# The first three loads of r change their issuing queue, from SyncE to ScalarE

## The chip, the cores and the metric

The kernel runs on one core of a Trainium2 chip. The metric is the device time of one execution in microseconds (us): the median over runs.

## The reference

Two layers follow each other. The first is a linear attention with a decaying state (4 batches, 8 heads, 768 steps, head size 48); the second is a two-layer MLP with a squared ReLU over the 3072 tokens, of width 384 and inner width 2048.

```
state = zeros(B, H, D, D)
for t in range(S):
    cur = einsum('bhd,bhe->bhde', u * k[:, :, t], v[:, :, t])
    y[:, :, t] = einsum('bhd,bhde->bhe', r[:, :, t], state + cur)
    state = w * state + einsum('bhd,bhe->bhde', k[:, :, t], v[:, :, t])
x = y as (B*S, H*D)
h = maximum(x @ moe_w_in, 0)
out = (h * h) @ moe_w_out
```

## The kernel before

The 768 steps are cut into 6 chunks of 128, and with 4 batches that makes 24 units, numbered i, unit i being chunk i // 4 of batch i % 4. For every unit three tiles of 128 steps x 8 heads x 48 values in float32 are loaded (`ld.r.i`, `ld.k.i`, `ld.v.i`, 192 KB each). A head's row of 48 values is contiguous in memory and nothing longer is, so each of these loads is 1024 pieces of 192 bytes.

Per unit the work is:

- `kh` and `rh` (L320, L323) scale k by `Wkhat` and r by `Wt` into a bf16 tile `rk`. Both factors are powers of the decay w. They are made once, at the start: the load `w` brings w's row (L256), `shw` spreads it over the partitions on VectorE (L265), and ScalarE forms `logw`, `Wkhat` and `Wt` (L271, L274, L277).
- `P0`, `P1`, `du`, `dv` (L326, L330, L333, L338) are the part with u.
- `T` transposes `rk` on TensorE (L347) and `Tc` copies the result to SBUF (L250). From unit 8 on a transposing DMA (`XB`, L353) does both.
- `A` is the 128x128 product of the two transposed tiles (L360), `Bm` masks it (L372), `Y` multiplies it and the state with v (L380, L382), and `U` makes the state's update (L391).
- `xs` adds Y and dv (L399), `X` transposes the sum (L417) and `xTc` copies it (L250); later units use a transposing DMA (`xX`, L424).
- `F1`, `re`, `sq`, `F2` are the MLP (L433, L441 and L443, L448 to L452, L460), for one unit or a pair of units at a time; `os` and `out` store the result.

The weights of the MLP come in eight pieces. Of `moe_w_in`, four pieces of 768 KB in rows of 2 KB are loaded in float32 (`lW.0.s`, L301) and cast to bf16 (`cW.0.s`: L250 on ScalarE, L252 on GpSimd). The four of `moe_w_out` are loaded by GpSimd's queue with a cast on the way (`W.1.s`, L317; 384 KB as written); a tiny copy, `gate` (L311), that reads a loaded v tile stands ahead of each and holds it back.

Nothing is scheduled by a program: the string `ORDER` lists all steps of all engines, and each engine carries out its own steps in the order in which they stand there. A step reads `name.numbers:engine/buffer`, with A for ScalarE, D for VectorE, G for GpSimd, P for TensorE and S for SyncE. SyncE (SP in the profile) only issues DMAs, and nearly all of them are its own: 24 loads each of r, k and v, the four `lW`, the stores and the transposing DMAs. ScalarE issues one DMA in the whole kernel, the row of w.

The r, k and v tiles have five buffers each; a load from the sixth unit on waits until its buffer's last readers are done. DMAs from SyncE and ScalarE draw their completion semaphores from eight that are reused in turn, so that the ninth such DMA also waits until the first one has landed, and so on.

Of the kernel before, what the change touches and what calls it, by code (L numbers as in the profile page):

```python
# [17 lines left out]
POOLS = dict(ldr=5, ldk=5, ldv=5, ws=4, rk=6, P0=4, dv=3, vb=8, rkT=6, bank=4, bankH=2, bankO=2, Bm=6, xs=3, xT1=2, xT2=2, xT4=1, hr=6, hq=28, os=3, ts=2)  # L18
GATES = [[('v', 1), ('v', 1), ('v', 1), ('v', 1)], [('v', 1), ('v', 1), ('v', 3), ('v', 3)]]
ORDER = """  # L20
tab:A ld.k.1:S/0 ld.r.0:S/0 ld.r.1:S/1 ld.k.0:S/1 w:A lW.0.2:S/0 u:S lW.0.0:S/1 lW.0.1:S/2 ld.v.1:S/0 shw:D ld.k.2:S/2
logw:A Wk:A ld.v.3:S/1 P0.1:D/0 Wt:A kh.1:G/0 ld.r.2:S/2 kh.0:D/1 rh.1:D rh.0:G ld.k.4:S/3 T.1:P/0 cW.0.2:A ld.v.4:S/2
P0.0:D/1 T.0:P/1 Tc.1:A/0 shu:D ld.r.3:S/3 P1.0:D Tc.0:A/1 P1.1:D A.1:P/2/3 du.0:D/0 cW.0.0:A A.0:P/0/1 du.1:D/1
ld.v.0:S/3 cW.0.1:G Bm.0.0:D/0 ld.k.3:S/4 Bm.0.1:D/1 vb.1:A/0 lW.0.3:S/3 Bm.1.1:D/2 kh.2:G/2 Bm.1.0:D/3 ld.v.2:S/4
gate.1.0:G vb.3:D/1 Y.1:P/0 wc:S U.1:P/1 gate.1.1:G dv.1:D ld.r.4:S/4 xs.1:D/0 P0.2:G/2 X.1:P/3 ld.k.5:S/0 vb.4:A/2
# [82 lines left out]
    ld=["{0}{1}"],  # L108
    lW=["ws{0}{1}"], kh=["rk{0}"], P0=["P{0}"], du=["dv{0}"], vb=["vb{0}"], T=["bT{0}"], Tc=["rkT{0}"], XB=["rkT{0}"],
# [413 lines left out]
```

## Time and profile before

| | |
|---|---|
| median of 13 runs | 183.52 us (181.42 to 185.4) |
| the profiled execution's own time | 184.97 us |
| its span in the profile | 183.3 us |
| TensorE matmul busy (PE) | 156.7 us, 86% |
| VectorE / ScalarE / GpSimd busy | 124.3 / 120.8 / 112.9 us |
| granted TensorE clock | full speed in all 40 slices |
| packets on the queue of SyncE (q1) | 103912, 27.81 MB |
| packets on the queue of ScalarE (q10) | 8, 0.01 MB |

The span is the time between the first and the last recorded instruction. The execution's own time has 1.67 us more around it. Rows of a timeline give the start and the duration in us, the engine and line, the tile written and the tile read, the number of instructions merged into the row, and in brackets the idle time before the row with what ended it. "SPq" and "ACTq" are DMA issues of SyncE and ScalarE: their duration is how long the issuing takes the queue's sequencer, not how long the data take. The DMA share is that of 16 DMA engines; it counts each packet with a duration of its own and so can come out above 100%.

### The profile page before, as it was taken

How to read it: one execution, taken by the hardware profiler on the slowest of the kernel's cores; microseconds unless marked ns; L12 is line 12 of the kernel's file. 1: busy time of each engine (PE TensorE's matmuls, PEld its weight loads, DVE VectorE, ACT ScalarE, POOL GpSimd, SP SyncE). 2: the span in 40 equal slices, each digit the busy share in tenths (PEclk: the TensorE clock that was granted, in tenths of full speed). 3: DMA queues.
4: the chain of work that ended last, by engine and by line, in shares of the span. 5: the costliest groups of instructions: out<-in, count | busy, mean ns of one | idle time of the engine just before them, and what ended most of it. 6: DMA issues, size and time to landing. Idle time of an engine off the chain costs nothing.

```text
span 183.3 us, 4254 instructions
## 1 busy us (share of the span) xinstructions
PE 156.7 (86%) x1640; PEld 118.5 (65%) x1640; DVE 124.3 (68%) x220; ACT 120.8 (66%) x209; POOL 112.9 (62%) x125
## 2 busy tenths in 40 slices
PE   0143677999799999878999998999999999999992
PEld 0032656768577777646777867668687787777761
DVE  3767289768868898876868587587984777723220
ACT  2374549678489857815759659749667776677852
POOL 3406687955596599882899996969989940000000
PEclk9999999999999999999999999999999999999999
DMA  5999999989799899989899899899755325220112
GB/s 111 267 337 183 190 250 200 209 151 200 155 212 231 200 179 223 146 195 199 189 179 209 181 191 192 168 214 150 165 117 123 60 66 122 68 64 0 50 40 86
DMA packets 106052, 29.66 MB, mean 162 GB/s; under 512 B 99368, under 2 KB 104496, under 8 KB 106032
## 3 DMA queue, kind: packets, MB, share of 16 engines
q1 hardware_dynamic: 103912, 27.81, 71.7%
q0 software_dynamic: 2112, 1.57, 5.8%
q8 instruction: 13, 0.21, 0.5%
q14 instruction: 7, 0.06, 0.1%
q10 hardware_dynamic: 8, 0.01, 0.0%
HBM read 20.46 MB, written 4.72 MB: 137 GB/s over the span
## 4 chain that ended last, share of the span: by engine, by line
PE 60%; DMA 19%; SPq 11%; ACT 3%; issue 2%; DVE 2%; POOL 1%; DVEq 0%; ACTq 0%
PE bank L460 27%; PE bank L433 26%; DMA ldv<-in_v_dram 13%; SPq L296 9%; DMA W<-in_moe_w_out_dram 5%; PE bank L382 2%; DMA xT<-xs 2%; PE bank L360 2%; ACT hr L441 2%; SPq L301 2%; PE bank L380 2%; PE bank L391 1%; DVE du L333 1%; ACT vb L250 1%; DVE rk L323 1%
## 5 line engine op out<-in xcount | busy, mean ns | idle before, releaser
L433 PE MATMUL bank<-xT,W 128*128 128x256 bf16 (+1 forms) x624 | 73.9, 268 | 4.1 <-ACT W L250 1.4
L460 PE MATMUL bank<-W,hq 128*128 128x384 bf16 x384 | 73.3, 326 | 1.4 <-DMA W<-in_moe_w_out_dram 0.9
L433 PEld LDWEIGHTS <-W 128*128 128x128 bf16 x624 | 57.0, 100 | 14.6 <-issue 2.4
L441 ACT ACTIVATE hr<-bank 128x512 bf16<-128x512 f32 x86 | 50.7, 595 | 23.3 <-PE bank L433 21.9
L460 PEld LDWEIGHTS <-hq 128*128 128x128 bf16 x384 | 36.1, 98 | 20.1 <-issue 1.3
L450 DVE TENSOR_TENSOR hq<-bank,hr 128x512 bf16<-128x512 f32 x37 | 25.4, 689 | 28.7 <-ACT hr L441 28.7
L448 ACT ACTIVATE hq<-hr 128x512 bf16<-128x512 bf16 x57 | 35.7, 629 | 1.9 <-DVE hr L443 0.4
L372 DVE TENSOR_TENSOR Bm<-bank,maskJT 128x512 bf16<-128x512 f32 x48 | 31.0, 681 | 3.3 <-PE bank L360 3.3
L326 POOL TENSOR_TENSOR P<-ldr,ldk 128x384 f32<-128x384 f32 x22 | 23.9, 1087 | 4.1 <-DMA ldr<-in_r_dram 4.1
L320 POOL TENSOR_TENSOR rk<-ldk,Wkhat 128x384 bf16<-128x384 f32 x21 | 21.3, 1015 | 4.4 <-ACT Wkhat L274 4.1
L323 POOL TENSOR_TENSOR rk<-ldr,Wt 128x384 bf16<-128x384 f32 x20 | 21.7, 1084 | 2.7 <-DMA ldr<-in_r_dram 2.7
L330 POOL TENSOR_TENSOR P<-P,ub 128x384 f32<-128x384 f32 x20 | 21.8, 1088 | 1.2
L250 ACT CAST vb<-ldv 128x384 bf16<-128x384 f32 x22 | 11.2, 509 | 17.1 <-DMA ldv<-in_v_dram 17.0
L412 POOL TENSOR_TENSOR S0W<-ts,WLm 128x384 bf16<-128x384 f32 x14 | 14.2, 1017 | 10.7 <-DVE ts L409 10.6
L399 DVE TENSOR_TENSOR xs<-bank,dv 128x384 bf16<-128x384 f32 x24 | 13.3, 552 | 7.2 <-PE bank L382 6.6
L250 ACT COPY os<-bank 128x384 f32<-128x384 f32 x22 | 10.4, 472 | 7.0 <-PE bank L460 6.7
L382 PE MATMUL bank<-vb,Bm 128*128 128x48 bf16 x192 | 11.4, 185 | 4.1 <-DVE Bm L372 2.6
L347 PE MATMUL bank<-identity,rk 128*128 128x128 bf16 x64 | 6.2, 254 | 9.0 <-POOL rk L320 7.6
L382 PEld LDWEIGHTS <-Bm 128*128 128x128 bf16 x192 | 9.8, 97 | 5.7 <-DVE Bm L372 2.9
L338 DVE TENSOR_TENSOR dv<-ldv,du 128x384 f32<-128x384 f32 x19 | 13.1, 692 | 0.3
L333 DVE TENSOR_REDUCE du<-P 128x8 f32<-128x384 f32 x24 | 12.9, 543 | 0.1
L360 PE MATMUL bank<-rkT 48*128 48x128 bf16 x192 | 8.6, 225 | 3.6 <-ACT rkT L250 2.4
(57 smaller groups left out, 111.9 us busy)
## 6 DMA issues: line engine op xcount, KB each, us to landing
ldk<-in_k_dram SPq DMA_DIRECT2D x24, 192.0 KB, 3.8
ldr<-in_r_dram SPq DMA_DIRECT2D x24, 192.0 KB, 3.7
ldv<-in_v_dram SPq DMA_DIRECT2D x24, 192.0 KB, 5.0
out_dram<-os SPq DMA_DIRECT2D x24, 192.0 KB, 2.9
ws<-in_moe_w_in_dram SPq DMA_DIRECT2D x4, 768.0 KB, 7.2
W<-in_moe_w_out_dram POOLq DMA_DIRECT2D x4, 384.0 KB, 7.9
rkT<-rk SPq DMA_TRANSPOSE x16, 3.5
xT<-xs SPq DMA_TRANSPOSE x16, 3.1
```

Of the source, the lines that this page charges most:

```text
L250: e.copy(o, a)
L320: e.tensor_mul(rk[slot[f"rk{i}"]][:, 1, :, 0:D], loaded("k", i), Wkhat)
L323: e.tensor_mul(rk[slot[f"rk{i}"]][:, 0, :, 0:D], loaded("r", i), Wt2)
L326: e.tensor_mul(P0b[slot[f"P{i}"]], loaded("r", i), loaded("k", i))
L330: e.tensor_mul(t, t, ub)
L372: e.tensor_mul(Bmb[slot[f"Bm{i}{h}"]], heads(bank(f"bA{i}{h}"), 128), mask_b)
L382: e.matmul(y[:, hc, D * h : D * (h + 1)], m[h][:, hc, :], vb[:, 2 * hc + h, :], start=(c == 0), stop=True, skip_group_check=True,)
L433: e.matmul(hp[:, fi, :], W1[f // 4][:, c, 128 * (f % 4) : 128 * (f % 4 + 1)], xt[:, c, :], start=(c == 0), stop=(c == CCH - 1), skip_group ...
L441: e.activation(hr, hp, AF.Relu)
L448: e.activation(hq, hr, AF.Square)
L450: e.tensor_mul(hq, bank(f"bH{g},{s}", "bH"), hr)
L460: e.matmul(bank(f"bO{i}", "bO")[:, 0:d_model], hqb[slot[f"hq{g},{f // m}"]][:, at : at + L], W2[q][:, f % 4, :], start=(f == 0), stop=(f = ...
```

## The change

`ld.r.0`, `ld.r.1` and `ld.r.2` are given to engine A. Buffers and places in `ORDER` stay as they are. No other line of the kernel changes.

```diff
 ORDER = """
-tab:A ld.k.1:S/0 ld.r.0:S/0 ld.r.1:S/1 ld.k.0:S/1 w:A lW.0.2:S/0 u:S lW.0.0:S/1 lW.0.1:S/2 ld.v.1:S/0 shw:D ld.k.2:S/2
-logw:A Wk:A ld.v.3:S/1 P0.1:D/0 Wt:A kh.1:G/0 ld.r.2:S/2 kh.0:D/1 rh.1:D rh.0:G ld.k.4:S/3 T.1:P/0 cW.0.2:A ld.v.4:S/2
+tab:A ld.k.1:S/0 ld.r.0:A/0 ld.r.1:A/1 ld.k.0:S/1 w:A lW.0.2:S/0 u:S lW.0.0:S/1 lW.0.1:S/2 ld.v.1:S/0 shw:D ld.k.2:S/2
+logw:A Wk:A ld.v.3:S/1 P0.1:D/0 Wt:A kh.1:G/0 ld.r.2:A/2 kh.0:D/1 rh.1:D rh.0:G ld.k.4:S/3 T.1:P/0 cW.0.2:A ld.v.4:S/2
```

SyncE's list loses three DMAs: it now begins `ld.k.1`, `ld.k.0`, `lW.0.2`, `u`, `lW.0.0`, `lW.0.1`, `ld.v.1`, `ld.k.2`, `ld.v.3`, `ld.k.4`. ScalarE's list now begins `tab`, `ld.r.0`, `ld.r.1`, `w`, `logw`, `Wk`, `Wt`, `ld.r.2`, `cW.0.2`, `Tc.1`. The order on TensorE, VectorE and GpSimd is the same. The semaphores are dealt out anew, which gives some of the early DMAs another one to wait for: `ld.k.2` waited for the row of w to land and now waits for `lW.0.2` to land, and `ld.r.2` waits for `ld.r.0`.

## Prediction

> **What bounds the kernel now.** I read the chain of waits first, for the stage in which the moved loads lie.
>
> ```profile
> 7.50 3.68 SPq L296
> ...
> 11.22 3.45 SPq L296
> ...
> 21.02 6.22 DMA ldv<-in_v_dram
> ...
> 27.29 0.50 POOL vb L252
> 27.79 0.75 POOL W L317
> 28.54 8.95 DMA W<-in_moe_w_out_dram
> ...
> 37.53 0.81 PE bank L460 x4
> ```
>
> Up to 21 us the chain is SyncE issuing DMAs back to back. Then come a v tile (ld.v.2), a vb on GpSimd, the second piece of moe_w_out, and TensorE, which from 37.5 us on has few gaps. Whoever stops here would call SyncE's issuing the bound and expect the three issues to come off the end. So I read what the 16 DMA engines did meanwhile (stretches; columns: PE, PEld, DVE, ACT, POOL busy, granted clock, DMA share, GB/s).
>
> ```profile
> 2.00:6.00 4.00, 0.00 (x0) 0.00 (x0) 1.31 (x6) 0.72 (x3) 0.48 (x2) 1.00 1.04 203
> 6.00:10.00 4.00, 1.29 (x11) 1.03 (x12) 3.83 (x6) 1.00 (x2) 2.26 (x2) 1.00 0.90 286
> 10.00:14.00 4.00, 1.59 (x22) 1.06 (x21) 2.18 (x5) 3.55 (x4) 0.00 (x0) 1.00 1.05 348
> 14.00:16.00 2.00, 0.41 (x8) 0.14 (x4) 1.49 (x3) 1.62 (x2) 1.09 (x1) 1.00 0.71 142
> 16.00:20.00 4.00, 2.09 (x23) 1.80 (x24) 2.97 (x6) 0.00 (x1) 3.36 (x5) 1.00 1.06 209
> ```
>
> From 2 us on the DMA engines are full but for two small gaps: 10% of 6 to 10 us (0.4 us) and 29% of 14 to 16 us (0.6 us). SyncE is held back by them: it issues a 192 KB load in 0.45 to 0.95 us, the engines need 1.0 us for its 1024 packets, and the 3.68 and 3.45 us of two equal loads are SyncE waiting for room. The stage is bound by DMA packets, whoever issues them.
>
> The third view is the timeline of the engines that the moved loads meet.
>
> ```profile
> 4.71 0.58 DVE L265 STREAM_SHUFFLE wb<-wrow 128x384 f32<-128x384 f32 x1
> ...
> 6.41 0.60 ACT L277 ACTIVATE Wt<-logw,tcol 128x384 f32<-128x384 f32 x1
> ...
> 10.45 1.47 ACT L250 CAST W<-ws 128x1536 bf16<-128x1536 f32 x1 [3.44 <-DMA ws<-in_moe_w_in_dram]
> 11.83 1.92 ACT L250 COPY rkT<-bank 128x1024 bf16<-128x1024 bf16 x2
> ...
> 20.57 0.47 ACT L250 COPY xT<-bank 128x384 bf16<-128x384 bf16 x1
> ```
>
> Row w lands at 4.69 us, Wt is done at 7.01, and then ScalarE has nothing until lW.0.2 lands at 10.45.
>
> **The change part by part.** *SyncE loses three issues.* They took 0.56, 0.77 and 0.67 us, with 0.04 between: 2.1 us of sequencer. What hides them is the full DMA engines: the packets ahead of ld.v.2 and of the last lW are the same ones, r's included, so they land when they did. Worth 0, and 2.1 us if the cover were not there.
>
> *The same 3072 packets go through a second queue.* Two queues share an engine; no row of before has two full loads side by side, the nearest are the queues of GpSimd (q0, packets of 768 B) and SyncE (q1, 192 B). In 33.25 to 34.25 us the DMA view counts:
>
> ```profile
> q0 software_dynamic: 192, 0.15, 93.6%
> q1 hardware_dynamic: 189, 0.04, 33.1%
> ```
>
> So they go one for one, a pair in 16 / 190 = 84 ns of an engine. Alone, q0 has 207 packets in 32.0 to 32.75 us, 58 ns each; q1 alone has 5389 in 16 to 21 us, 15 ns each. A pair costs 84 where the two alone make 73: 11 ns more, no gain. Bounds: 192 packets of r on each engine x 11 ns = 2.1 us lost at most; at best both gaps of the second view are filled, 1.0 us won. Most r packets pair with equal k packets, which are nearer to the 15 ns row, with nothing lost or won; the rest, about 100 per engine (r2 and a tail of r1) against 2 KB packets, could lose 1.1 us, about what the gaps could give. I take 0 and keep -1.0 and +2.1.
>
> [...]
>
> *The row of w moves behind r0 and r1 in its own queue.* Its issue goes from 1.37 to about 2.3 us (0.9 + 0.56 + 0.77), and its packet now lies behind 128 packets of r on its engines. k1 and k0 (128 packets) go in the other queue from 2.0 us. If both queues start together, all is through after 256 x 15 ns = 3.8 us, and w lands at 5.8: 1.1 later. If ScalarE's queue starts l us later, 67 l packets of r1 are left when k is done, and each of these then takes turns with a 2 KB packet of lW (97 ns in the records): 67 l x 112 ns = 7.6 l, less the 1.0 l that the lead already counts, w at 5.8 + 6.6 l. The first packets left 1.1 us after the start of k1's issue, and 2.0 us after that of w; both I read from the packet records. So l lies between 0.1 and 1.0, and w between 6.5 and 12.4. I take l = 0.4, w at 8.4, 3.7 us later, since r0's issue starts beside k1's and shares only the making of packets with it.
>
> [...]
>
> Who waits for w: shw, logw, Wkhat, Wt, all kh and rh, T.1 and T.0. Their covers, one behind another: T.1's transposes are through by about 9.8 us and Tc.1 starts at 11.83, behind cW.0.2 (2.0 us); X.1 ends at 18.73 + 0.50 = 19.23 and xTc.1 starts at 20.57, because ScalarE waits for ld.v.4 (1.3 us); and
>
> ```profile
> 28.17 1.51 PE L433 MATMUL bank<-xT,W 128*128 128x128 bf16 x24 [1.43 <-ACT W L250]
> ```
>
> TensorE waits 1.4 us for cW.0.3, whose piece is one of those DMAs that do not move. In all 4.7 us. A delay of 3.7 costs 0. P0.1, which waited 0.63 us for r1 at 5.93, is part of the same delay.
>
> *ld.r.2 stands between Wt and cW.0.2 on ScalarE.* The issue takes 0.67 to 1.08 us (w's) there, inside the idle 3.44 us; without that cover, or with w very late, cW.0.2, Tc.1 and Tc.0 move by as much. Its wait for r0 has long been met. r2 was issued at 14.72 and used at 18.65; now it is issued before 11 us and, pair by pair with 2 KB packets (64 x 112 ns = 7.2 us), lands by 18. GpSimd's wait of 0.64 us for it at 18.69 goes, but GpSimd waits 1.38 us for ld.v.0 at 22.39, so nothing arrives earlier behind it.
>
> *ld.k.2 waits for lW.0.2 instead of w.* That is until 10.4 us on SyncE, with ld.v.3, ld.k.4 and all later loads behind it; its issue already took until 11.18, and lW.0.0, lW.0.1 and ld.v.1 (about 110 packets per engine) keep the DMA engines at work. 0; if the issue were as slow after the wait as before, up to 3 us of SyncE.
>
> Sum: 0 + 0 + 0 + 0 + 0 on the profiled 184.97 us; that execution lies 1.45 us above the median, so I state the median, 183.5 us. I call differences over 0.5% (0.92 us) faster or slower, about what a measurement of this kernel can tell from no change.
>
> **The rivals.** *SyncE was the bound.* Then lW.0.3, ld.v.2 and with them moe_w_out come up to 2.1 us earlier: 181.4 us; with only the gaps filled 1.0, 182.5. For it: the chain of waits and the two gaps. Against: a DMA share of 1.04 to 1.06 and the two long issues. Chance 0.25.
>
> *The row of w is the new start.* Its price is (6.6 l + 1.1) - 4.7: it decides from l = 0.55 us on, costs 1.3 at l = 0.75 (184.9 us) and 3.0 at l = 1.0 (186.5 us). For it: w's own 2.0 us to its first packet, and the alternation one for one. Against: w's issue lay among three of SyncE's. The mixing loss, above 0 on its own, works in the same direction. Chance 0.35 in all.
>
> *The forecast:* both effects disappear in covers, 0.40, by itself 182.8 to 184.3.
>
> **How the numbers follow.** Half of the faster rival's cases lie near 182.5, and of the slower one most near 185; about 0.1 is left out at each end with 182.1 to 185.5. Faster 0.25, same 0.40, slower 0.35.
>
> **What would show it.** In the profile after: SyncE's long issues are still there, and about as long together; ScalarE's queue q10 has 3072 packets more; shw starts between 6 and 9 us; cW.0.2 starts within 1 us of 10.45; F1.1.0 within 0.7 us of 21.10; the piece of moe_w_out lands for TensorE near 37.5. I am wrong if the packets of ld.v.2 arrive over 1 us earlier or later than 27.2, or if F1.1.0 starts after 22 us and TensorE is still behind at 37.5.

## The result, and the profile after

The changed kernel takes 181.52 us (median of 11 runs, 179.86 to 184.34), the kernel before 183.78 us in the same comparison (48 runs). The ratio is 0.9906 [0.9872, 0.9939], with its 95% interval: faster by 0.9%, or 1.7 us. Some executions are in a slower state (of after those of 184.34 and 183.87 us, with a granted clock of 0.991 against 0.997 to 1.0), and all ratios here compare the others only, so that they differ a little from those of the medians. The forecast was 183.5 us with a range of 182.1 to 185.5, and "no change" as its likeliest case. Both missed.

The profiled execution of after took 179.86 us (span 178.1). That of before, on which the prediction worked, took 184.97 us and lies above its own median, so that a difference of these two traces shows too much. A second profile of before, taken with the experiments, has a time of 181.52 us and a span of 179.7; where the size of a difference matters I use it ("the second profile of before", run e0 below), and beside it a second profile of after (a1_after, span 177.7).

Up to 40 us, the chain of waits of after has lost SyncE, the v tile and the pieces of moe_w_out, which are all still in that of the second profile of before. Up to 21 us it is now the row of w and the work on TensorE and VectorE behind it; the one long piece of it is

```profile
2.10 5.57 DMA wrow<-in_w_dram
```

The same stretches as in the prediction (PE, PEld, DVE, ACT, POOL busy, granted clock, DMA share, GB/s), after:

```profile
2.00:6.00 4.00, 0.00 (x0) 0.00 (x0) 0.64 (x3) 0.09 (x1) 0.48 (x2) 1.00 1.19 229
6.00:10.00 4.00, 0.00 (x0) 0.00 (x0) 1.42 (x4) 1.55 (x4) 0.33 (x1) 1.00 1.04 382
10.00:14.00 4.00, 2.50 (x24) 1.83 (x24) 3.97 (x6) 3.29 (x5) 3.46 (x3) 1.00 1.19 304
14.00:16.00 2.00, 0.61 (x8) 0.35 (x8) 2.00 (x4) 1.87 (x3) 0.91 (x2) 1.00 1.40 218
16.00:20.00 4.00, 0.86 (x13) 0.66 (x14) 3.90 (x9) 0.51 (x1) 2.53 (x5) 1.00 1.16 207
```

The last two columns are what changed: 229 GB/s for 203 in the first stretch and 382 for 286 in the second. In the second profile of before these two were

```profile
2.00:6.00 4.00, 0.00 (x0) 0.00 (x0) 1.63 (x6) 0.61 (x2) 0.49 (x2) 1.00 1.08 213
6.00:10.00 4.00, 1.85 (x16) 1.48 (x16) 3.48 (x6) 1.54 (x3) 2.63 (x2) 1.00 0.99 346
```

so the DMA engines carry more in the same time against this execution too. In 14 to 16 us, the second gap of the prediction, the second profile of before also carries less, 188 GB/s to 218 after:

```profile
14.00:16.00 2.00, 0.00 (x0) 0.00 (x0) 2.00 (x4) 0.76 (x2) 2.00 (x2) 1.00 0.95 188
```

The timeline of the start, after:

```profile
0.81 1.08 SPq L296 DMA_DIRECT2D ldk<-in_k_dram  x2
0.84 1.22 ACTq L296 DMA_DIRECT2D ldr<-in_r_dram  x2
1.93 1.02 SPq L301 DMA_DIRECT2D ws<-in_moe_w_in_dram  x1
2.10 1.52 ACTq L256 DMA_DIRECT2D wrow<-in_w_dram  x1
7.80 0.58 DVE L265 STREAM_SHUFFLE wb<-wrow 128x384 f32<-128x384 f32 x1
8.64 0.37 SPq L296 DMA_DIRECT2D ldk<-in_k_dram  x1
8.98 0.45 ACTq L296 DMA_DIRECT2D ldr<-in_r_dram  x1
9.05 3.44 SPq L296 DMA_DIRECT2D ldv<-in_v_dram  x1
9.49 0.60 ACT L277 ACTIVATE Wt<-logw,tcol 128x384 f32<-128x384 f32 x1
10.00 1.46 ACT L250 CAST W<-ws 128x1536 bf16<-128x1536 f32 x1
20.50 0.48 ACT L250 COPY xT<-bank 128x384 bf16<-128x384 bf16 x1 [1.88 <-PE bank L417]
21.11 2.77 PE L433 MATMUL bank<-xT,W 128*128 128x128 bf16 x24
26.59 1.51 PE L433 MATMUL bank<-xT,W 128*128 128x128 bf16 x24
```

The row of w is spread at 7.80 instead of 4.71 us, and cW.0.2 (10.00), xTc.1 (20.50) and F1.1.0 (21.11) hardly move against the first profile of before. But the 24 matmuls of F1 that waited for cW.0.3 there start at 26.59 instead of 28.17.

From the landing marks of the trace (16 for each load; no engine is named with them, and I take them as one for each of the 16 DMA engines; a load counts as landed with the last of them) comes the table that the rest of this text is about, in us:

| landed | before | second profile of before | after | a1_after |
|---|---|---|---|---|
| lW.0.2, last engine | 10.43 | 9.56 | 8.63 | 8.35 |
| lW.0.1, median engine | 13.67 | 12.86 | 12.48 | 12.33 |
| lW.0.1, last engine | 14.86 | 13.74 | 12.79 | 12.52 |
| ld.v.2, median engine | 26.31 | 25.01 | 24.05 | 23.50 |
| ld.v.2, last engine | 27.24 | 25.56 | 24.90 | 24.60 |

At lW.0.1 it is the last engine that gains most; at ld.v.2 the median engine gains even more than the last (1.5 and 1.0 us, a1_after against the second profile of before). So the lag does not stay with one engine: all of them do later work earlier. What lies between is the stretch of 14 to 16 us: it carries 127 to 188 GB/s in the seven kernels of this text with r0 and r1 on SyncE's queue and 201 to 218 in the nine with two queues. That the lag makes this gap, by holding SyncE back while most engines have nothing left, fits these rows; no run shows it by itself.

How this reaches the end is seen at TensorE, whose instructions stand in one order in all kernels. Against the second profile of before, the 144th matmul of F1 starts 0.7 us earlier in a1_after (45.6 for 46.3 us), the 240th 1.0 us (71.3 for 72.3) and the 300th 2.1 us (90.9 for 93.0); the end comes 2.0 us earlier. The largest step lies at 78 us, where the second profile of before has a wait for a transposing DMA (issued by SyncE at 74.58 us):

```profile
74.58 1.26 SPq L353 DMA_TRANSPOSE rkT<-rk  x1
77.80 0.40 PE L360 MATMUL bank<-rkT 48*128 48x128 bf16 x8 [1.12 <-DMA rkT<-rk]
```

In a1_after SyncE is 2.2 us further on,

```profile
72.35 1.26 SPq L353 DMA_TRANSPOSE rkT<-rk  x1
```

and TensorE's waits after 45 us name no rkT any more. The first profile of before has that wait too (1.20 us), after doesn't. So in this pair the lead seems to be kept in the DMAs, whose engines are nearly full up to 120 us (a share of 0.95 or more in each stretch of 20 us behind the first), and TensorE collects it in portions. Other pairs take other portions: f1 below is 1.8 us ahead of its twin f2 at the 144th matmul (45.2 for 47.0 us) and 0.9 at the 300th.

### The profile page after: what moved, and what is told of

Same layout as the page of the kernel before. It is cut to its first block, busy times and chain, and to the rows that moved or that the text cites. A ratio compares the mean times of both kernels' runs of the same rounds, so it can differ in the third digit from the quotient of the medians.

```text
span 178.1 us, 4254 instructions
## 1 busy us (share of the span) xinstructions
PE 156.2 (88%) x1640; PEld 118.3 (66%) x1640; DVE 125.0 (70%) x220; ACT 119.7 (67%) x209; POOL 113.1 (63%) x125
## 4 chain that ended last, share of the span: by engine, by line
PE 73%; DVE 10%; DMA 8%; ACT 3%; issue 3%; DVEq 0%
PE bank L433 32%; PE bank L460 31%; DMA ldv<-in_v_dram 4%; DMA wrow<-in_w_dram 3%; PE bank L382 2%; PE bank L360 2%; DVE Bm L372 2%; ACT hr L441 2%; PE bank L380 2%; DMA xT<-xs 2%; PE bank L391 2%; PE bank L347 1%; DVE P L330 1%; DVE dv L338 1%; DVE du L333 1%
## 5 line engine op out<-in xcount | busy, mean ns | idle before, releaser
L320 POOL TENSOR_TENSOR rk<-ldk,Wkhat 128x384 bf16<-128x384 f32 x21 | 21.9, 1044 | 8.3 <-ACT Wkhat L274 7.2
L323 POOL TENSOR_TENSOR rk<-ldr,Wt 128x384 bf16<-128x384 f32 x20 | 21.2, 1062 | 1.0 <-DMA ldr<-in_r_dram 1.0
L338 DVE TENSOR_TENSOR dv<-ldv,du 128x384 f32<-128x384 f32 x19 | 14.1, 744 | 0.3
L347 PEld LDWEIGHTS <-rk 128*128 128x128 bf16 x64 | 5.0, 114 | 11.9 <-POOL rk L320 11.1
```

What stands on the lines that cost most here:

```text
L320: e.tensor_mul(rk[slot[f"rk{i}"]][:, 1, :, 0:D], loaded("k", i), Wkhat)
L323: e.tensor_mul(rk[slot[f"rk{i}"]][:, 0, :, 0:D], loaded("r", i), Wt2)
```

## The experiments

**Which of the three loads counts.** e0_before_again is the kernel before, for a second profile. e1_r0_r1_only moves two of the loads, e2_r2_only the third.

```diff
 e1_r0_r1_only
-ld.r.0:S/0 ld.r.1:S/1
+ld.r.0:A/0 ld.r.1:A/1
 e2_r2_only
-ld.r.2:S/2
+ld.r.2:A/2
```

> The kernel before, profiled once more. It asks whether the slower 2 KB stage of its first profile (286 GB/s from 6 to 10 us, lW.0.2 landing at 10.4 us with two late engines, against 382 GB/s and 8.6 us in the changed kernel) belongs to the kernel or to that one execution. If to the kernel: again under 300 GB/s from 6 to 10 us, lW.0.2 after 10 us. If to the execution: near 370 GB/s, lW.0.2 near 8.8 us, ld.v.2 landing about 1.5 us sooner than 27.2, and a span of about 181.

> r0 and r1 on ScalarE's queue, r2 back on SyncE's. Theory 'two queues side by side get more packets through an engine': the overlap of 2 to 6 us stays, that of 12 to 15 us goes; half of the gain of 1.0 to 2.3 us, about 182.8 us against 183.8 of before. Theory 'SyncE two issues ahead': two thirds of the gain, about 182.3. Theory 'the gain is r2, which no longer stands in SyncE's list ahead of ld.k.4 and ld.v.4': nothing left, 183.8. Row w lands near 7.7 us in any case.

> Only r2 on ScalarE's queue. Theory 'two queues side by side': the overlap of 12 to 15 us alone, about half of the gain, 182.8 us. Theory 'SyncE ahead': a third, 183.1. Theory 'r2 out of SyncE's list': all of it, 181.6. Row w lands at 4.7 as before.

e0 took 181.52 us; before on that chip has a median of 181.23 (23 runs). Its 346 GB/s and its lW.0.2 at 9.56 us lie between the two cases of the expectation: a part of what the first profile showed was that execution's own, and a part is the kernel's. e1: 179.51 us, ratio 0.9955 [0.9912, 0.9997]. e2: 180.99 us, ratio 0.9989 [0.9943, 1.0034], no gain that could be told from none. In 6 to 10 us e1 moves 386 GB/s as after does, e2 only

```profile
6.00:10.00 4.00, 1.79 (x16) 1.48 (x16) 3.46 (x5) 1.45 (x4) 2.63 (x2) 1.00 0.97 306
```

and ld.v.2 lands at 24.59 us in e1 and at 26.00 in e2. By these two views the effect belongs to r0 and r1, that is to the first six microseconds. The two times do not decide it, as their intervals overlap; f1 below, which also leaves r2 on SyncE, does.

**The slower rival on purpose.** In e3_w_first the row of w goes back to the head of ScalarE's queue. Thereby r0 and r1 get there late.

```diff
-tab:A ld.k.1:S/0 ld.r.0:A/0 ld.r.1:A/1 ld.k.0:S/1 w:A lW.0.2:S/0
+tab:A w:A ld.k.1:S/0 ld.r.0:A/0 ld.r.1:A/1 ld.k.0:S/1 lW.0.2:S/0
```

> All three r loads on ScalarE's queue, but the row of w ahead of them, so that it need not wait behind r0 and r1. If the late w (7.7 us) costs nothing, as the covers say: the time of the changed kernel, 181.5. If it costs, in the changed kernel, up to 1 us: about 180.7. If r0 and r1 come late now and cost in their place: 182 or more.

184.69 us, ratio 1.0253 [1.019, 1.0315]: slower by 2.5%, or 4.5 us. r0 is issued at 2.50 us, and most of its packets and those of r1 are left when the 2 KB packets of lW.0.2 begin. From then on they share the engines, not evenly at first: in 7 to 9.5 us ScalarE's queue (q10) has 1210 packets and SyncE's (q1) 317. In 9 to 12 us the DMA view counts

```profile
q1 hardware_dynamic: 517, 1.00, 92.8%
q10 hardware_dynamic: 485, 0.09, 16.0%
```

517 and 485 packets, nearly one for one. r1 lands at 13.95 us, and the rest of T.1 waits for it:

```profile
16.65 1.46 PE L347 MATMUL bank<-identity,rk 128*128 128x128 bf16 x12 [8.45 <-DVE rk L323]
```

F1.1.0 follows at 27.59 us. So the slower rival's mechanism, small packets that wait their turn beside large ones, exists, though here it is r0 and r1 that come late and not w; in the changed kernel, where r0 is issued at 0.84 us, they land by 6.59 us (8.01 in a1_after).

**Two queues, or a smoother order?** In the changed kernel a tail of r1 stood against the first 2 KB packets, and it was thinkable that this order did the good. f1 and f2 put another small load, ld.v.1, ahead of lW.0.2; f1 with r0 and r1 on ScalarE, f2 with all on SyncE. a1_after is the changed kernel again, and g1_more_on_act also gives ld.k.4 and ld.r.3 to ScalarE.

```diff
 f1_v1_ahead_two_queues
-ld.r.0:S/0 ld.r.1:S/1 ld.k.0:S/1 w:A lW.0.2:S/0 u:S lW.0.0:S/1 lW.0.1:S/2 ld.v.1:S/0
+ld.r.0:A/0 ld.r.1:A/1 ld.k.0:S/1 w:A ld.v.1:S/0 lW.0.2:S/0 u:S lW.0.0:S/1 lW.0.1:S/2
 f2_v1_ahead_one_queue
-ld.r.0:S/0 ld.r.1:S/1 ld.k.0:S/1 w:A lW.0.2:S/0 u:S lW.0.0:S/1 lW.0.1:S/2 ld.v.1:S/0
+ld.r.0:S/0 ld.r.1:S/1 ld.k.0:S/1 w:A ld.v.1:S/0 lW.0.2:S/0 u:S lW.0.0:S/1 lW.0.1:S/2
 g1_more_on_act, beside the change itself
-ld.k.4:S/3
+ld.k.4:A/3
-ld.r.3:S/3
+ld.r.3:A/3
```

> The changed kernel once more, beside the ones that follow. About 0.9% under the kernel before of the same chip. If its smooth start into the 2 KB loads belongs to the kernel: no 2 KB packet over 200 ns before 14 us again (about 30 in each profile in which SyncE issues r0 and r1), lW.0.2 landing before 8.8 us, over 370 GB/s from 6 to 10 us.

> r0 and r1 on ScalarE's queue, and on SyncE's ld.v.1 ahead of lW.0.2, so that r1 is through before the first 2 KB packet and no small packets take turns with it. Theory 'the tail of r1 lets the 2 KB loads start smoothly': slow 2 KB packets come back (20 or more over 200 ns), lW.0.2 takes over 2.3 us from the landing of ld.v.1, and the time is that of its one-queue twin or less by only the 0.3 to 0.4 us of the faster small packets. Theory 'two queues are faster by themselves, or descriptors written long before they are used are': no slow packets, 1.5 us or more under its one-queue twin. Row w lands near 6.2 us.

> The twin: all on SyncE's queue, ld.v.1 ahead of lW.0.2. Both theories: about 30 slow 2 KB packets, time within 0.5% of before (ld.v.1 early is not needed, each lW 1 us later, behind which 2 us of cover lie).

> The changed kernel with ld.k.4 and ld.r.3 on ScalarE's queue too, so that 192 B loads run on both queues from 11 to 17 us. Theory 'small packets of two queues go through an engine up to a quarter faster': ld.v.2 lands 0.5 to 1 us sooner than in the changed kernel, time 0.5 us lower. Theory 'only the start into the 2 KB loads counts': ld.v.2 and the time as in the changed kernel. If the issues hold ScalarE up (room in its queue), cW.0.0 starts over 1 us later and the time rises.

Before on that chip: 181.09 us (23 runs). a1: 179.63 us, 0.9885 [0.983, 0.994]. f1: 180.09 us, 0.9901 [0.9864, 0.9937]. f2: 181.52 us, 1.0022 [0.998, 1.0063]. g1: 179.58 us, 0.9896 [0.9856, 0.9936]. This order is worth nothing by itself (f2), two queues are worth the 1% with it too (f1; the intervals of f1 and f2 do not touch), and further loads on the second queue bring nothing more (g1; ld.v.2 lands at 24.55 us, in a1 at 24.60). The stretch of 6 to 10 us is, in f1 and then in f2,

```profile
6.00:10.00 4.00, 0.00 (x0) 0.00 (x0) 1.84 (x5) 1.98 (x4) 0.76 (x1) 1.00 1.09 356
```

```profile
6.00:10.00 4.00, 1.46 (x13) 1.20 (x14) 3.46 (x4) 0.84 (x2) 2.26 (x2) 1.00 0.97 284
```

**Does the early arithmetic slow the loads?** The two lines just shown differ in something else too: where w is early, TensorE, VectorE and GpSimd are at work while the 2 KB packets pass. Six kernels end before unit 8's first transposing DMA (only the first third of the work is done), so that start and time stand closer together; the whole kernel has no run of these edits.

```diff
 c4_cut_young_two_queues: two columns of w ahead of lW.0.2, so that SyncE issues it later
-ld.r.0:S/0 ld.r.1:S/1 ld.k.0:S/1 w:A lW.0.2:S/0
+ld.r.0:A/0 ld.r.1:A/1 ld.k.0:S/1 w:A wc:S lW.0.2:S/0
 c5_cut_late_w_one_queue: the row of w behind lW.0.0 on SyncE
-ld.k.0:S/1 w:A lW.0.2:S/0 u:S lW.0.0:S/1 lW.0.1:S/2
+ld.k.0:S/1 lW.0.2:S/0 u:S lW.0.0:S/1 w:S lW.0.1:S/2
 c6_cut_early_w_two_queues: the row of w early, on SyncE
-ld.r.0:S/0 ld.r.1:S/1 ld.k.0:S/1 w:A lW.0.2:S/0
+ld.r.0:A/0 ld.r.1:A/1 w:S ld.k.0:S/1 lW.0.2:S/0
 c2_cut_order_one_queue: one queue, k0 ahead of r1 and r2 ahead of v3
-ld.r.0:S/0 ld.r.1:S/1 ld.k.0:S/1 w:A
+ld.r.0:S/0 ld.k.0:S/1 ld.r.1:S/1 w:A
```

> The kernel before, ended ahead of its first transposing DMA (about a third of the work; it leaves out all of units 8 to 23 that stands behind that point, and writes only the first stores). It is the yardstick for the cut kernels beside it. All theories: an early stage like that of the whole kernel, about 30 2 KB packets over 200 ns before 14 us, span near 62 us.

> Cut in the same place and leaving out the same work. r0 and r1 on ScalarE's queue, and on SyncE's the two small wcol loads ahead of lW.0.2, so that lW.0.2 is issued about 1 us before its turn. Theory 'lead' (2 KB packets are slow when issued about 1 us or less before their turn): 20 or more slow ones, the gain on the cut kernel before falls to 0.4 us. Theory 'two queues as such' and theory 'early arithmetic' (the row of w is late here, near 7.5): 2 or fewer, and 1 us or more of gain stays.

> Cut in the same place and leaving out the same work. All on SyncE's queue, with the row of w issued by SyncE behind lW.0.0: it lands near 9 us and the arithmetic of 5 to 10 us moves behind it. Theory 'early arithmetic' (VectorE, GpSimd and TensorE at work beside the 2 KB loads make their packets slow): 5 or fewer slow packets before 9 us, and up to 1 us faster than the cut kernel before. Theories 'lead' and 'two queues as such': about 30, time that of the cut kernel before or up to 1 us over it.

> Cut in the same place and leaving out the same work. r0 and r1 on ScalarE's queue, and the row of w on SyncE's behind ld.k.1, landing near 4.5 us: the arithmetic lies at 5 to 10 us as in before. Theory 'early arithmetic': 20 or more slow 2 KB packets, and most of the gain is lost. Theories 'lead' and 'two queues as such': 2 or fewer, and 1 us or more under the cut kernel before.

> The changed kernel, cut in the same place as the cut kernel before (and leaving out the same work). It measures the gain at that place: if the gain is made in the first 25 us and only handed on, 1.5 to 2.2 us under 65.7, as in the whole kernel; 63.7.

> Cut in the same place, leaving out the same work. All on SyncE's queue, but in the order in which the loads land in the changed kernel (k1, r0, k0, r1, then r2 ahead of ld.v.3). Theory 'two queues as such': no gain, 65.7 within 0.6 us. Theory 'it is the order of the loads': 63.7.

Ratios are to the whole kernel before; each cut kernel has four or five runs. On the first chip: c0 65.71 us (0.3546 [0.3499, 0.3593]), c4 63.87 (0.3468 [0.3421, 0.3516]), c5 67.08 (0.3664 [0.3623, 0.3704]), c6 63.61 (0.3469 [0.3434, 0.3503]). On the second: c1 63.71 (0.3503 [0.3454, 0.3551]), c2 63.76 (0.3524 [0.3495, 0.3553]). These intervals are wide: by them c5 is slower than c0, c4 and c6 are probably faster, and c1 and c2 can be told neither from c0 nor from each other.

c5 has no arithmetic at all in 6 to 10 us and moves 308 GB/s (c0, with it, 341), c6 has all of it and moves 381:

```profile
6.00:10.00 4.00, 0.00 (x0) 0.00 (x0) 0.00 (x0) 0.00 (x0) 0.00 (x0) 1.00 0.93 308
```

```profile
6.00:10.00 4.00, 1.20 (x10) 0.94 (x11) 3.77 (x6) 2.21 (x3) 2.26 (x2) 1.00 1.03 381
```

So in these runs the arithmetic does not slow the loads. Why c5 is slower than c0 is another matter: its w landed at 12.71 us, far behind the 9 us that I expected. c6 has its w 3.0 us earlier than after has (4.67 for 7.67 us) and is not faster than the others with two queues: the late w of the change costs nothing that could be measured, though the intervals leave room for some 1 us. In c4, SyncE issues lW.0.2 at 3.44 us, nearly as late as in c0 (3.75; c1 1.92), and yet lW.0.1 lands at 12.98 us (c0 14.50, e0 13.74, c1 12.84): SyncE's early issuing is not what the gain needs. c2 told nothing by its time: its interval holds c0 and c1, and its 63.76 us is the number that was expected of the order. So the time does not exclude that k0 ahead of r1 and r2 ahead of v3 are worth something on one queue; the landings below do show c2 with the lag of one queue.

**The loads by themselves.** m1 and m2 (and m3 below; one execution each) contain nothing but loads, in stages that begin when all of the stage before has landed and been read; m2 has the stages in another order. No layer is computed.

> The loads of the first stage by themselves, with no other work of the kernel (all arithmetic but one-element copies is left out): k1, r0, r1, k0, the three lW and v1 on SyncE's queue, the same with r0 and r1 on ScalarE's, the three lW alone, the four small loads on one and on two queues, and both orders with v1 ahead of the lW; seven stages, each begun when all of the one before has landed, four rounds. Theory 'the small packets are faster on two queues': the stage of four small loads takes 0.5 to 0.7 us less on two queues, and the whole stage is shorter by the same. Theory 'the 2 KB stage is smoother behind two queues': the whole stage is shorter by 1 us or more, the lW alone take as long as behind one queue. Theory 'both are effects of the other work of the kernel': no stage differs by 0.3 us.

> The same seven stages in another order (two queues ahead of one), four rounds, so that no stage owes its time to the one before it. The same differences as in the other order, by every theory.

From the first to the last packet, the stage k1 r0 r1 k0, three pieces of moe_w_in, v1 took 11.8 to 12.4 us in m1 and 11.3 to 12.7 in m2 with all on SyncE; with r0 and r1 on ScalarE it took 10.7 to 10.9 and 11.0. With v1 ahead of the pieces: 12.0 to 13.4 and 12.0 to 12.7 on one queue, 10.7 to 11.0 and 10.8 on two. Nothing else runs here, so the gain is one of the loads alone, 1.4 us of about 12. Of the stages with few loads some ran into the next one and gave no number.

In the one-queue stages 13 to 35 of the 1152 packets of 2 KB took over 200 ns, with two queues 0 to 3. But the pieces are also issued 1.6 us earlier there. m3 separates the two: its stage two_late delays SyncE's pieces by three tiny loads, and one_seven puts seven small loads ahead of them.

```diff
 m3_loads_alone_later, stage two and then two_late
-ld.k.1:S/0 ld.r.0:A/0 ld.r.1:A/1 ld.k.0:S/1 lW.0.2:S/0 lW.0.0:S/1 lW.0.1:S/2 ld.v.1:S/0
+ld.k.1:S/0 ld.r.0:A/0 ld.r.1:A/1 ld.k.0:S/1 u:S wc:S lW.0.2:S/0 lW.0.0:S/1 lW.0.1:S/2 ld.v.1:S/0
```

> The kernel makes no layer at all: it only repeats stages of loads, and each stage begins when the one before has landed and been read. Kinds of stage: 'one' (k1 r0 r1 k0, three pieces of moe_w_in, v1, all issued by SyncE); 'two' (r0 and r1 issued by ScalarE); 'two_late' (as 'two', but SyncE also issues three tiny loads, u and two columns of w, ahead of the three pieces, so that it issues the pieces 1 to 2 us later); 'one_seven' (seven small loads, k1 r0 r1 k0 v1 k2 r2, ahead of the three pieces, all by SyncE, so that the pieces are issued longer before their packets' turn); 'two_seven' (the same with the three r by ScalarE). Theory A, late issuing: the pieces are slow when SyncE issues them shortly before their turn; then 'two_late' has slow 2 KB packets (ten or more over 200 ns a stage) and its 1152 packets of 2 KB take 7.4 us or more, and 'one_seven' has nearly none and takes 6.6 to 7.0 us for them. Theory B, the second queue as such: 'two_late' has none and takes 6.6 to 7.0 us, 'one_seven' has ten or more and takes 7.4 us or more. Both: 'one' 7.0 to 8.4 us with 15 to 35 slow packets, 'two' and 'two_seven' 6.6 to 7.1 us with 0 to 3.

Means of four stages each, in us from the stage's first packet:

| stage | first piece issued | whole stage | lW.0.1 at the median engine | at the last engine | last behind median | 2 KB packets over 200 ns |
|---|---|---|---|---|---|---|
| one | 1.61 | 12.19 | 10.77 | 11.95 | 1.18 | 17 to 32 |
| two | 0.05 | 10.80 | 10.33 | 10.63 | 0.30 | 0 to 1 |
| two_late | 1.61 | 11.16 | 10.71 | 11.00 | 0.29 | 17 to 37 |

Each theory got one half. The slow packets come with late issuing: two_late has them, as c4 has (20; after has none and a1_after two). But the time does not come from the slow packets: two_late needs 6.93 us for its 2 KB packets, two 6.90, one 7.98. one_seven was meant to issue long ahead and did not: the packets of its pieces began 0.65 to 1.16 us after the end of their issue, much as in one. It has 18 to 30 slow packets and 14.19 us, two_seven none and 12.70.

The columns "median" and "last" settle where the time is. The median engine gains 0.38 us (10.71 to 10.33) when SyncE issues earlier and almost nothing through the second queue by itself (10.77 to 10.71). The last engine loses its lag of 0.9 us (1.18 to 0.29) through the second queue alone. Single stages vary: in the 16 one-queue stages of m1 and m2 the lag at lW.0.1 goes from 0.34 to 2.31 us, and in those with two queues none is over 0.60. The stretches of m3 show it directly: the ends of one stage "one", one "two" and one "two_late" (columns: DVE and POOL busy, granted clock, DMA share, GB/s):

```profile
99.30:100.30 1.00, 0.00 (x0) 0.00 (x0) 1.00 1.04 393
100.30:101.30 1.00, 0.14 (x1) 0.00 (x0) 1.00 1.06 259
101.30:102.30 1.00, 0.00 (x0) 0.00 (x0) 1.00 0.18 42
```

```profile
86.20:87.20 1.00, 0.00 (x0) 0.00 (x0) 1.00 1.07 340
87.20:88.20 1.00, 0.27 (x3) 0.00 (x0) 1.00 0.65 131
```

```profile
131.30:132.30 1.00, 0.00 (x0) 0.00 (x0) 1.00 1.04 372
132.30:133.30 1.00, 0.03 (x1) 0.00 (x0) 1.00 0.96 203
```

With one queue, a whole microsecond passes with a DMA share of 0.18, the work of about three engines of 16, while most of the others have nothing left. With two queues v1, the last load, lands on its first and its last engine within 0.26 to 0.50 us, with one queue within 0.99 to 1.65. And in the kernels: behind the median engine, the last one lands lW.0.1 0.88 to 1.63 us late in all seven kernels with r0 and r1 on SyncE (e0 0.88, before 1.19, f2 1.47, c0 1.63, c2 1.06), and 0.19 to 0.73 us in all nine with two queues (a1 0.19, f1 0.22, after 0.31, c4 0.29, c6 0.73). A small lag at lW.0.1 is not enough for a fast kernel, though: e3, where r comes late, has 0.71.

Why the engines drift apart behind one queue is open. The two other orders of the small loads keep the lag (f2, c2), so does a start without arithmetic (c5, 1.15), and late issuing does not bring it (two_late, c4). The lag is there at the first piece already (1.09 us at lW.0.2 in e0) and does not grow in the next two. The trace doesn't say which engine carried a packet, so that I could not follow the late ones.

## Why the prediction was wrong, and where it was right

**The step that failed** is "the same 3072 packets go through a second queue", taken at 0 within -1.0 to +2.1. It measures -0.95 us in the loads alone (two_late against one, at the last engine), and -0.7 in the kernel: the lag of lW.0.1 goes from 0.88 in e0 to 0.19 in a1. The size is inside the bounds, and the best case that I named, both gaps filled, is what the stretches show (after, a DMA share of 1.04 in 6 to 10 us and of 1.40 in 14 to 16). What I did not have is a reason why they should fill, and so I took 0. I counted packets of an average engine and found that a pair gains nothing, which the median engine of m3 confirms (0.06 us). But a load lands with its last engine, and no line of my sum was about that one. The trace of before had the evidence: lW.0.2 landed at 8.56 on the median engine and at 10.43 on the last, and I read only the latter.

**SyncE's three issues, "worth 0"**, were mis-sized by a little: issuing 1.6 us earlier is worth 0.38 us in m3. The cover held for the rest, as far as m3, c4 and g1 tell. SyncE's long issues are still there (ld.v.3's takes 3.44 us at 9.05 us, ld.v.4's 1.88), though shorter than the 3.68 and 3.45 of before. That they are waits for room is an inference that no trace shows: of the queue's data packets issued by then, 2443 and 1504 had not begun when the 3.68 and the 3.45 us of before ended, and up to 2619 at the end of the other issues before 22 us. Together the two terms make 1.3 us in m3 (11.95 to 10.63), 1.2 in the landing of lW.0.1 (13.74 to 12.52) and 1.0 in that of ld.v.2; I had 0. The sign of being wrong that I had named came true: ld.v.2 landed at 24.90 us, over 1 us earlier than 27.2.

**Right:** the stage of before is bound by its DMA packets, but not "whoever issues them", and what they gain arrives at the end. Not so in the stage of after, where up to 21 us the chain runs through w and VectorE. The start of ScalarE's queue: the first packets of r leave 0.43 us after those of k (I took 0.4; that the two issues share only the making of packets was my assumption, and no run shows it), and w lands at 7.67 us (I had 8.4; in its formula 67 l x 112 ns is 7.5 l and not 7.6, which changes nothing). ScalarE's queue has 3120 packets more. The covers of w held; the price of the late w against a comparable execution is that F1.1.0 starts at 21.11 and not at 19.58 us, and by the 144th matmul nothing of it is left. ld.k.2's new wait ends at 8.64 us, and no run shows a cost (in e1 SyncE issues it from 6.33 us on, and ld.v.2 lands at 24.59 us, in a1 at 24.60). ld.r.2 lands at 15.59 us (I had "by 18"), its issue lies beside ScalarE's Wkhat (8.98 to 9.43 us), and it is worth nothing that could be told (e2).

**The rivals.** "SyncE was the bound" named 181.4 to 182.5 us, and its price is near what came, by luck: the gaps did fill, but its mechanism is some 0.4 of the 1.7 us (m3), c4 keeps the gain with a late issue, and g1, which takes two more issues from SyncE, gains nothing. "The row of w is the new start" was right in the chain (it begins with w now) and wrong in the price: l was 0.43, below the 0.55 from which it was to decide. With r0 behind w (e3) the same taking of turns costs 4.5 us, there through late r0 and r1.

**The chance.** 0.40 for "no change" rested on a sum of zeros in which the one term with no row of its own had bounds of 3 us.

## What to carry to other kernels

A load counts here as landed with its last DMA engine (at lW.0.1 0.88 us behind the median one in e0, 0.19 in a1): look at the spread of a load's landings over the engines before you call a transfer stage bound by its packets. Where many loads of small packets stand in one queue ahead of large ones that something waits for, try every other one of them on a second, idle queue, from the first packet on; here it paid when the second queue started together with the first (0.43 us apart, 1% faster) and not when it started late (r0 issued 1.7 us later, 2.5% slower). And give a term that no row shows its own chance in the forecast, not the middle of its bounds.

## What was not expected of the hardware

- Behind one queue the DMA engines drift apart: in the kernels the last one lands lW.0.1 0.9 to 1.6 us behind the median, with r0 and r1 on a second queue 0.2 to 0.7. It is not so for every load: in a1_after r1 itself lands 1.9 us behind its median engine.
- In m3 small packets went faster from two queues. From the 1000th to the 3000th packet of 192 bytes it takes 1.48 to 1.51 us in the stages of m3 with two queues, and 1.63 to 1.74 us with one.
- Packets of 2 KB over 200 ns come with a short time between the end of the issue and the first packet: 0.65 to 1.42 us in m3 wherever they were many, 1.69 to 2.43 us where there were none or one. They cost no time there.
- Two queues don't always take turns. In e3 they did in 9 to 12 us, 517 to 485, and not in 7 to 9.5 us, 317 to 1210. In after, ld.r.2 was issued at 8.98 us, and yet the DMA view of 8.9 to 12 us, while the 2 KB packets passed, has SyncE's queue alone:

```profile
q1 hardware_dynamic: 772, 1.16, 104.3%
```

r2's packets came after these, in 12 to 15.6 us. What decides it, no run here shows.
